# A routed attention kernel: the first block's rows turned after the last unit's first value products, and the routing probabilities stored as 18 rows

## The chip, the cores and the metric

One Trainium2 chip, one of its cores. The metric is device microseconds of one execution. The kernel before takes 1200.1 us, the median of three runs (1199.29 to 1203.38).

## What is computed

Three layers, one after the other, in float32: attention with pooled queries, a dense layer with a gate, and a routed layer with eight experts of which each token uses one.

```python
def _moe2_ref(x, w_gate, w_local, w1, w2):
    logits = np.einsum('bsd,de->bse', x, w_gate)
    local_gate = 1.0 / (1.0 + np.exp(-np.einsum('bsd,de->bse', x, w_local).squeeze(-1)))
...
            fresh_e = int(np.argmax(logits[b, s]))
            e = fresh_e if s == 0 or local_gate[b, s] < 0.5 else prev_e
...
            p = np.exp(logits[b, s] - logits[b, s].max())
            p /= p.sum() + 1e-09
            h = np.maximum(x[b, s] @ w1[e], 0.0)
            out[b, s] = p[e] * (h @ w2[e])
```

The input `x` has 4 x 576 = 2304 tokens of 512 numbers; an expert's matrices are 512 x 1024 and 1024 x 512. A token keeps the expert of the token before it where its local gate is open. `p[e]` is the routing probability that this case is about.

## The kernel before

**Stages.** Attention runs over 32 heads, to about 640 us. The dense layer works in nine units of 256 tokens (`u` from 0 to 8): `hidden` (the up products and the squares), `gate` (the sigmoid factor), `value` (the down products) and `product`, which multiplies the two and stores 128 rows of `x2d` in DRAM. Each matrix product is made of three passes over a high and a low half of its operands (`PASSES`). For each unit, `logits`, `route1`, `route2`, `route3` and `route4` find the expert of each token and scatter the token numbers into a table `tbl` in DRAM, one list for each expert; route4 issues two table scatters, each of which waits for the one before.

**Blocks.** The routed layer then works in blocks of up to 512 tokens of one expert. The numbers of a block's tokens are loaded from `tbl` (`load_ids`), their rows are gathered from `x2d` in two pairs of 128 (`gather_x`), turned on TensorE and split into high and low halves (`transpose_x`: 8 transposes, two copies on ACT at L1057 and two subtractions on DVE at L1058), taken through `up` and `down`, scaled with the tokens' probabilities (`gather_p` reads them from `pd` in DRAM into `pg`; `finish` does the scaling at L1093) and scattered to the output (L1094). Weights come in pieces of 512 KB (`load_w`) into a ring of raw buffers, three for the first block and five later, and are split by ACT and DVE (`split_w`, L1010 and L1011), which frees the buffer for a later piece. Block 0 belongs to the expert with the most tokens of units 0 to 6; it is chosen early (`early`, L1242), so that its rows and weights come while units 7 and 8 are still in the dense layer. The other blocks are known only after unit 8 has been routed (`block_list`, `block_list2`).

**Order.** The order on every engine is written out by hand: an engine works through its instructions in the order in which the program issues them. What matters here are the lines from L1288 on, for the last unit (u = 8). They issue `gate(u, 0)`, then `transpose_x(0)` for the first 256 rows of block 0 and `gather_x(0, 2)` for the other 256, which go into the same buffer `xg0`; then `route2` of unit 7, the first weight split, and `value(u, 0)` in two halves with `route3` of unit 7 between them. `product(u, 0)`, the second split, `gate(u, 1)` and `route4` of unit 7 follow, and then the rest of unit 8, between the up products of block 0. The second `transpose_x(0)` stands at L1330.

At L1349 `probabilities()` computes the probabilities of all 2304 tokens in one tile `pe`, 128 partitions x 18 columns (token 128 t + p stands in partition p, column t), and stores it at once to `pd`, which is in token order: every number is a piece of 4 bytes by itself. The store is issued on SP behind the first five weight pieces of block 1 and the two `load_ids` for blocks 1 and 2. On POOL the rows of block 1 are gathered next (L1350) and then the probabilities of block 0 (L1351, L1352), which wait for the store. On TensorE `down(0, 2)` and `down(0, 3)` stand before the second half of block 0, whose rows are up at L1378 (`pair_up`), whose first half is scaled at L1382, and whose down products are at L1390 (`pair_down`). In between `next_x(0)` turns the rows of block 1. All engines load eight numbers into registers at L1355 and L1356, and SP 20 more at L1358, before the sixth weight piece of block 1 is loaded.

Of the kernel before, what the change touches and what calls it, by code (L numbers as in the profile page):

```python
# [16 lines left out]
P = 128  # L17
# [20 lines left out]
def kernel(  # L38
# [16 lines left out]
    nc = tc.nc  # L55
# [4 lines left out]
    NTOK = B * T  # L60
# [3 lines left out]
    NT = NTOK // P  # L64
# [12 lines left out]
    pd = dram.tile([NTOK + 1, 1], F32, name="pd")  # L77
# [11 lines left out]
    ident = cp.tile([P, P], F32, name="ident")  # L89
# [103 lines left out]
    for i in range(2):  # L193
        t = s1.tile([P, KT, 192], F32, name=f"V{i}")
# [402 lines left out]
    for a in range(NH):  # L597
        e = a == NH - 1
# [11 lines left out]
    for t in range(NS + 23):  # L610
        h, kt = divmod(t, KT)
        p = h // 2
# [52 lines left out]
        if t == NS + 3:  # L665
# [5 lines left out]
            p1, p23 = [pm.tile([P, DM], F32, name=n) for n in ("p1", "p23")]  # L671
# [80 lines left out]
    def gate(u, i, p_r):  # L752
        a = AB[1][u % 2]
        s = slice(P * i, P * i + P)
        n = 0
        for c in range(4):
            for wl, xl in PASSES:
                nc.tensor.matmul(p_r, lhsT=a[:, xl, c, s], rhs=wr[:, wl, c], start=(n == 0), stop=(n == 11))
                n += 1
        RG[u, i] = u2.tile([P, DM], F32, name="r", bufs=4)  # L760
        nc.scalar.activation(out=RG[u, i], in_=p_r, func=AF.Sigmoid)

    def value(u, i, p_v, fs=range(8)):
        s = slice(P * i, P * i + P)
        for f in fs:
            for n, (wl, xl) in enumerate(PASSES):
                nc.tensor.matmul(  # L767
                    p_v, lhsT=SQ[u, f // 2][:, xl, f % 2, s], rhs=wv[:, wl, f],
                    start=(f == 0 and n == 0), stop=(f == 7 and n == 2),
                )  # L770

    def product(u, i, p_v):
        x2 = RG.pop((u, i))
        nc.vector.tensor_tensor(out=x2, in0=p_v, in1=x2, op=ALU.mult)
        t = 2 * u + i
        nc.sync.dma_start(x2d[P * t : P * t + P, :], x2)
        TT[u, i] = x2
# [49 lines left out]
    def route2(u):  # L827
        kg = KG.pop(u)
        p1r = p1.rearrange("p (j f) -> p j f", j=2)
        for j in range(2):  # L830
            for i in range(2):
                nc.tensor.matmul(
                    p1r[0:1, j, P * i : P * i + P], lhsT=kg[:, j, i : i + 1], rhs=identb, start=True, stop=True
                )
        kr = rp.tile([1, 2, 256], BF16, name="krow")
        nc.scalar.activation(out=kr, in_=p1r[0:1], func=AF.Copy)
        er = KG[u] = rp.tile([1, 256], BF16, name="erow", bufs=2)
        nc.vector.tensor_tensor_scan(
            out=er, data0=kr[:, 0], data1=kr[:, 1], initial=0.0 if u == 0 else carry[0][:, 255:256],
            op0=ALU.mult, op1=ALU.add,  # L840
        )
        carry[0] = er
# [138 lines left out]
    def load_w(s):  # L981
        j, c = divmod(s, 8)
        if j > JX:
            return
        e = regs[j][0]
        t = raws[s % NRAW if j else s % 3]
        if c < 4:
            nc.sync.dma_start(
                t.rearrange("p (c f) -> p c f", c=4),
                w1[bass.ds(e, 1), :, 256 * c : 256 * c + 256].rearrange("o (c p) f -> p (o c) f", p=P),  # L990
            )
        else:
            c -= 4
            nc.sync.dma_start(
                t.rearrange("p (c f) -> p c f", c=2),
                w2[bass.ds(e, 1), 256 * c : 256 * c + 256, :].rearrange("o (c p) f -> p (o c) f", p=P),
            )

    def split_w(s, eng=None):
        j, c = divmod(s, 8)  # L1000
        if j > JX:
            return
        t = raws[s % NRAW if j else s % 3]
        if c < 4:
            w = W1B[j % 2][:, :, c]
            t = t.rearrange("p (c f) -> p c f", c=4)
        else:
            w = W2B[j % 2][:, :, 2 * c - 8 : 2 * c - 6]
            t = t.rearrange("p (c f) -> p c f", c=2)
        nc.scalar.activation(out=w[:, 0], in_=t, func=AF.Copy)  # L1010
        (eng or nc.vector).tensor_tensor(out=w[:, 1], in0=t, in1=w[:, 0], op=ALU.subtract)  # L1011

    def load_ids(j):
        if j <= JX:
            nc.sync.dma_start(
                ids[j % 4], tbl[bass.ds(regs[j][1], 512), :].rearrange("(i p) o -> p (i o)", p=P),
                allow_slow_non_contiguous=True,
            )


    def gather_x(j, t):
        if j > JX:
            return
        for i in range(2):
            ix = bass.IndirectOffsetOnAxis(ap=ids[j % 4][:, t + i : t + i + 1], axis=0)
            if j:
                nc.gpsimd.indirect_dma_start(out=XGB[j % 2][:, i], out_offset=None, in_=x2d, in_offset=ix)
            else:
                nc.gpsimd.indirect_dma_start(
                    out=XGB[0][:, i], out_offset=None, in_=x2d[0 : 256 * (NU - 2)], in_offset=ix,  # L1030
                    bounds_check=256 * (NU - 2) - 1, oob_is_err=False,
                )

    def gather_p(j, t):
        for i in range(t, t + 2):
            ix = bass.IndirectOffsetOnAxis(ap=ids[j % 4][:, i : i + 1], axis=0)
            nc.gpsimd.indirect_dma_start(out=pgs[j % 2][:, i : i + 1], out_offset=None, in_=pd, in_offset=ix)  # L1037
# [7 lines left out]
    def transpose_x(j, b=0):  # L1045
        if j > JX:
            return
        xt = XT[j % 2]
        for c2 in range(2):
            pt = BK[b][0][c2]  # L1050
            for c in range(2):
                for i in range(2):
                    cc = 2 * c2 + c
                    nc.tensor.transpose(
                        pt[:, c, P * i : P * i + P], XGB[j % 2][:, i, P * cc : P * cc + P], ident
                    )
            nc.scalar.activation(out=xt[:, 0, 2 * c2 : 2 * c2 + 2], in_=pt, func=AF.Copy)  # L1057
            nc.vector.tensor_tensor(  # L1058
                out=xt[:, 1, 2 * c2 : 2 * c2 + 2], in0=pt, in1=xt[:, 0, 2 * c2 : 2 * c2 + 2], op=ALU.subtract
            )  # L1060
# [18 lines left out]
    def down(j, g, tiles=(0, 1)):  # L1079
        w, hs = W2B[j % 2], sq[g]  # L1080
        for i in tiles:
            n = 0
            for f in range(2):
                for wl, xl in PASSES:
                    nc.tensor.matmul(  # L1085
                        py[i], lhsT=hs[:, xl, f, P * i : P * i + P], rhs=w[:, wl, 2 * g + f],
                        start=(g == 0 and n == 0), stop=(g == 3 and n == 5),
                    )
                    n += 1
# [113 lines left out]
    def probabilities():  # L1203
        ls = rp.tile([P, NT, E], F32, name="ls")
        nc.vector.tensor_tensor(
            out=ls, in0=L[:, :, 0:E], in1=mx.unsqueeze(2).to_broadcast([P, NT, E]), op=ALU.subtract
        )
        nc.scalar.activation(out=ls, in_=ls, func=AF.Exp)
        sm = rp.tile([P, NT], F32, name="sm")
        nc.vector.tensor_reduce(out=sm, in_=ls, axis=AX.X, op=ALU.add)  # L1210
        nc.vector.tensor_scalar(out=sm, in0=sm, scalar1=1e-9, scalar2=None, op0=ALU.add)
        nc.vector.reciprocal(out=sm, in_=sm)
        nc.vector.tensor_tensor(out=ls, in0=ls, in1=oh, op=ALU.mult)
        pe = rp.tile([P, NT], F32, name="pe")
        nc.vector.tensor_reduce(out=pe, in_=ls, axis=AX.X, op=ALU.add)
        nc.vector.tensor_tensor(out=pe, in0=pe, in1=sm, op=ALU.mult)
        nc.sync.dma_start(
            pd[0:NTOK].rearrange("(t p) o -> p (t o)", p=P), pe, allow_slow_non_contiguous=True
        )


    def first_block():
# [64 lines left out]

    u = NU - 1  # L1288
    gate(u, 0, py[0])
    transpose_x(0)  # L1290
    gather_x(0, 2)
    route2(u - 1)
    split_w(0)
    load_w(3)
# [1 line left out]
    route3(u - 1)  # L1296
    value(u, 0, py[1], range(4, 8))
    product(u, 0, py[1])
    split_w(1)
    load_w(4)  # L1300
    gate(u, 1, py[0])
# [44 lines left out]
        load_w(s)  # L1346
    load_ids(1)
    load_ids(2)
    probabilities()  # L1349
    gather_x(1, 0)  # L1350
    gather_p(0, 0)  # L1351
    gather_p(0, 2)  # L1352
    down(0, 2)
    down(0, 3)
    n0 = nc.values_load(lst0[:, 2:3], min_val=0, max_val=512)  # L1355
    nk = [nc.values_load(nks[:, i : i + 1], min_val=0, max_val=JX) if i != 4 else None for i in range(8)]  # L1356
    for j in range(3, JX + 1):
# [103 lines left out]
```

## Time and profile before

| what | value |
|---|---|
| median of three runs | 1200.1 us |
| the profiled execution | 1199.74 us, its span 1198.0 us |
| mean granted TensorE clock | 0.972 of 2.4 GHz |
| busy in the span | TensorE matmul 1080.2 us (90%), DVE 828.2 (69%), ACT 718.6 (60%), POOL 575.3 (48%) |
| DMA | 156.31 MB in 147348 packets, 62993 of them under 512 bytes |

All starts are microseconds from the start of the span. PE is TensorE's matmul, PEld its weight load, DVE VectorE, ACT ScalarE, POOL GpSimd, SP SyncE. A row of a timeline has the start, the duration of the merged group, the engine, the line, the operation, the tiles as out<-in, the shape and the count; in brackets stands how long the engine was idle just before it and what ended that. Ends of matmuls are modelled and a group's end overlaps the next one's start a little, so differences of starts are the safer measure. A "q" behind an engine's name means its instruction queue. A row of a window has its bounds and length, the busy time (and instructions) of PE, PEld, DVE, ACT and POOL in this order, the granted clock, the DMA share and the GB/s. A granted clock of 1.00 is TensorE's level of 2.4 GHz, 0.50 that of 1.2 GHz.

### The profile page before, as it was taken

Reading aid. Unit: us, or ns where it says so; the run is one execution under the profiler, and the core shown is the slowest. Engines: PE = TensorE matmul, PEld = TensorE weight load, DVE = VectorE, ACT = ScalarE, POOL = GpSimd, SP = SyncE. Lnnn points to the kernel's source line nnn. Section 1 sums busy time; section 2 is a strip of 40 time slices with the busy share of each in tenths; the row PEclk is TensorE's granted clock in tenths of the full one; section 3 lists DMA queues with packets and bytes.
Section 4 is the critical chain, followed back from the end, with each engine's and each line's share of the span. In section 5 each row is a group of like instructions: output and inputs, shape, how many; then the busy total and the mean of one; then the engine's idle time right before and its main releaser. Section 6 shows DMA issues by size and latency. Waiting matters only on the chain. (4 is left out here: it accounts for less than half of the span.)

```text
span 1198.0 us, 18084 instructions
## 1 busy us (share of the span) xinstructions
PE 1080.2 (90%) x6073; PEld 910.6 (76%) x6073; DVE 828.2 (69%) x1255; ACT 718.6 (60%) x1006; POOL 575.3 (48%) x392
## 2 busy tenths in 40 slices
PE   7899999999999999978999989897987999998875
PEld 6677777777777777767887878776776888876764
DVE  6888888888888888889955665685353544446544
ACT  5787777777777777767775444341333535446543
POOL 2556666666666666468734333342213514144233
PEclk9999999999999999998999999998897999999988
DMA  9166666656566564515520322203646756556765
GB/s 198 32 132 148 138 142 141 140 130 131 131 149 141 137 138 100 157 45 172 182 98 10 36 31 32 36 18 89 117 81 153 253 178 202 176 179 213 251 205 176
DMA packets 147348, 156.31 MB, mean 130 GB/s; under 512 B 62993, under 2 KB 115857, under 8 KB 146324
## 3 DMA queue, kind: packets, MB, share of 16 engines
q1 hardware_dynamic: 140836, 141.51, 47.4%
q0 software_dynamic: 6384, 13.15, 3.7%
q8 instruction: 73, 1.20, 0.5%
q14 instruction: 55, 0.45, 0.1%
HBM read 107.30 MB, written 15.58 MB: 103 GB/s over the span
## 5 line engine op out<-in xcount | busy, mean ns | idle before, releaser
L403 PE MATMUL pvt<-sr,V 128*128 128x288 f32 x1152 | 328.5, 409 | 31.4 <-ACT xc L416 14.7
L403 PEld LDWEIGHTS pvt<-sr,V 128*128 128x128 f32 x1152 | 202.1, 190 | 71.2 <-POOL sr L389 17.9
L345 PE MATMUL pt<-kw 128*128 128x288 f32 x1152 | 247.3, 337 | 5.5 <-DVE Mt L357 4.1
L389 POOL TENSOR_TENSOR sr<-sr,Mb 128x576 f32<-128x576 f32 x96 | 142.5, 1487 | 195.3 <-ACT Mb L380 159.5
L357 DVE TENSOR_TENSOR Mt<-Mt,pt 128x576 f32<-128x576 f32 x224 | 168.1, 750 | 76.2 <-ACT sr L349 74.3
L349 ACT ACTIVATE sr<-pt 128x576 f32<-128x576 f32 x288 | 181.5, 646 | 54.6 <-PE pt L345 52.4
L345 PEld LDWEIGHTS pt<-kw 128*128 128x128 f32 x1152 | 177.6, 189 | 34.8 <-DVE Mt L357 10.4
L396 ACT ACTIVATE sr<-sr 128x1728 f32<-128x1728 f32 x96 | 157.9, 1644 | 52.0 <-DVE sr L390 46.4
L390 DVE TENSOR_TENSOR sr<-sr,Mb 128x1152 f32<-128x1152 f32 x96 | 160.9, 1676 | 2.8 <-ACT Mb L380 2.8
L727 PE MATMUL ph<-a,wk 128*128 128x256 f32 x864 | 108.4, 286 | 0.9 <-ACT kr L745 0.4
L727 PEld LDWEIGHTS ph<-a,wk 128*128 128x128 f32 x864 | 106.5, 193 | 2.6 <-ACT kr L745 1.0
L767 PE MATMUL py<-kw,sq 128*128 128x512 f32 x312 | 84.3, 423 | 0.0
L1068 PE MATMUL ph<-a,wk 128*128 128x256 f32 x576 | 73.4, 288 | 6.3 <-PEq L1415 5.8
L1085 PE MATMUL py<-kw,sq 128*128 128x512 f32 x324 | 78.3, 398 | 0.0
L1068 PEld LDWEIGHTS ph<-a,wk 128*128 128x128 f32 x576 | 71.3, 195 | 8.8 <-issue 7.7
L871 POOL DMA_INDIRECT tbl<-tid,si x18 | 18.4, 1021 | 122.9 <-DMA tbl<-tid,si 67.2
L745 ACT ACTIVATE kr<-ph 128x512 f32<-128x512 f32 x36 | 21.3, 592 | 92.4 <-PE ph L727 57.2
L446 POOL TENSOR_TENSOR xo<-xc,t 64x576 f32<-64x576 f32 x32 | 73.1, 2283 | 1.2
L783 DVE CUSTOM_DVE_ANT_0 a<-r,wg 128x512 f32<-128x512 f32 x96 | 71.4, 744 | 3.1
L767 PEld LDWEIGHTS py<-kw,sq 128*128 128x128 f32 x312 | 62.1, 203 | 15.0 <-issue 0.2
L1085 PEld LDWEIGHTS py<-kw,sq 128*128 128x128 f32 x324 | 60.8, 189 | 14.5
L1037 POOL DMA_INDIRECT pg<-pd,ids x44 | 44.4, 1009 | 37.4 <-DMA pg<-pd,ids 15.7
(250 smaller groups left out, 1756.7 us busy)
## 6 DMA issues: line engine op xcount, KB each, us to landing
wraw<-in_moe_w_dram SPq DMA_DIRECT2D x101, 512.0 KB
kw<-Hk SPq DMA_DIRECT2D x224, 72.0 KB
ql<-in_q_dram SPq DMA_DIRECT2D x16, 576.0 KB
kl<-in_k_dram SPq DMA_DIRECT2D x64, 144.0 KB
V<-in_v_dram SPq DMA_DIRECT2D x128, 72.0 KB
kw<-Hq SPq DMA_DIRECT2D x112, 72.0 KB
kw<-kw SPq DMA_DIRECT2D x14, 576.0 KB
xTd<-xo SPq DMA_DIRECT2D x16, 288.0 KB
```

The costliest lines, as they stand in the source:

```text
L345: nc.tensor.matmul(pt[:, i, :HT], lhsT=lhs, rhs=qh[:, hl, hd, i, :], start=(hl == 0), stop=(hl == 1))
L349: nc.scalar.activation(out=Sg[h, kt], in_=ptt[h, kt][:, :, :HT], func=AF.Copy)
L357: nc.vector.tensor_tensor(out=Mt[h], in0=a, in1=pt[:, :, :HT], op=ALU.max)
L389: nc.gpsimd.tensor_tensor(out=s[:, 0], in0=s[:, 0], in1=Mb[h], op=ALU.subtract)
L390: nc.vector.tensor_tensor(out=s[:, 1:3], in0=s[:, 1:3], in1=Mb[h].unsqueeze(1).to_broadcast([P, 2, T]), op=ALU.subtract)
L396: nc.scalar.activation(out=s, in_=s, func=AF.Exp, scale=scale)
L403: nc.tensor.matmul(pvt[h][:, i, :HT], lhsT=V[(h // 2) % 2][:, kt, c : c + P], rhs=Sg[h, kt][:, i], start=(kt == 0), stop=(kt == KT - 1),)
L446: nc.gpsimd.tensor_tensor(out=xo[p].rearrange("p (i t c) -> p i c t", i=2, c=9)[a], in0=y[a], in1=t2[a], op=ALU.mult)
L727: nc.tensor.matmul(pt[:, i], lhsT=wk[:, wl, g, c, P * i : P * i + P], rhs=a[:, xl, c], start=(n == 0), stop=(n == 11))
L767: nc.tensor.matmul(p_v, lhsT=SQ[u, f // 2][:, xl, f % 2, s], rhs=wv[:, wl, f], start=(f == 0 and n == 0), stop=(f == 7 and n == 2),)
L1068: nc.tensor.matmul(pt[:, i], lhsT=w[:, wl, g, c, P * i : P * i + P], rhs=x[:, xl, c], start=(n == 0), stop=(n == 11))
L1085: nc.tensor.matmul(py[i], lhsT=hs[:, xl, f, P * i : P * i + P], rhs=w[:, wl, 2 * g + f], start=(g == 0 and n == 0), stop=(g == 3 and n == 5),)
```

## The change

`transpose_x(0)` and `gather_x(0, 2)` of the last unit move from behind `gate(u, 0)` to behind `product(u, 0)`, ahead of the second weight split. `probabilities()` only computes; a new function `store_p` turns the 128 x 18 tile on TensorE to 18 rows of 128, copies them from PSUM (`p23`) into a part of the tile `ls` that is free by then, and stores 18 rows of 512 bytes. It is issued behind `down(0, 3)`, and the two `gather_p` behind it; their order on POOL's queue, after `gather_x(1, 0)`, stays.

```diff
--- before.py
+++ after.py
@@ -1214,9 +1214,14 @@
         pe = rp.tile([P, NT], F32, name="pe")
         nc.vector.tensor_reduce(out=pe, in_=ls, axis=AX.X, op=ALU.add)
         nc.vector.tensor_tensor(out=pe, in0=pe, in1=sm, op=ALU.mult)
-        nc.sync.dma_start(
-            pd[0:NTOK].rearrange("(t p) o -> p (t o)", p=P), pe, allow_slow_non_contiguous=True
-        )
+        return pe, ls
+
+
+    def store_p(pe, ls):
+        nc.tensor.transpose(p23[0:NT, 0:P], pe, ident)
+        row = ls.rearrange("p t e -> p (t e)")[0:NT, 0:P]
+        nc.vector.tensor_copy(row, p23[0:NT, 0:P])
+        nc.sync.dma_start(pd[0:NTOK].rearrange("(t p) o -> t (p o)", p=P), row)
 
 
     def first_block():
@@ -1287,8 +1292,6 @@
 
     u = NU - 1
     gate(u, 0, py[0])
-    transpose_x(0)
-    gather_x(0, 2)
     route2(u - 1)
     split_w(0)
     load_w(3)
@@ -1296,6 +1299,8 @@
     route3(u - 1)
     value(u, 0, py[1], range(4, 8))
     product(u, 0, py[1])
+    transpose_x(0)
+    gather_x(0, 2)
     split_w(1)
     load_w(4)
     gate(u, 1, py[0])
@@ -1346,12 +1351,13 @@
         load_w(s)
     load_ids(1)
     load_ids(2)
-    probabilities()
+    pe, ls = probabilities()
     gather_x(1, 0)
+    down(0, 2)
+    down(0, 3)
+    store_p(pe, ls)
     gather_p(0, 0)
     gather_p(0, 2)
-    down(0, 2)
-    down(0, 3)
     n0 = nc.values_load(lst0[:, 2:3], min_val=0, max_val=512)
     nk = [nc.values_load(nks[:, i : i + 1], min_val=0, max_val=JX) if i != 4 else None for i in range(8)]
     for j in range(3, JX + 1):
```

## Rows read from the trace of the kernel before

**Rows 1.** Windows, routed stage: busy us by engine (instructions), clock, DMA share, GB/s.
```profile
930.00:1092.00 162.00, 157.57 (x947) 137.19 (x945) 81.22 (x88) 79.47 (x107) 60.23 (x54) 1.00 0.61 195
1092.00:1198.00 106.00, 76.90 (x433) 64.79 (x432) 53.05 (x54) 50.80 (x65) 34.85 (x31) 0.93 0.69 214
```

**Rows 2.** PE's timeline, 827 to 850: start, us, line, tiles, count, idle before.
```profile
827.29 2.93 PE L758 MATMUL py<-wr,a 128*128 128x512 f32 x12
837.23 0.45 PE L1054 MATMUL ptx<-ident,xg 128*128 128x128 f32 x1 [7.00 <-DMA xg<-x2d,ids]
837.95 1.75 PE L1054 MATMUL ptx<-ident,xg 128*128 128x128 f32 x7 [0.28 <-DMA xg<-x2d,ids]
...
845.10 3.07 PE L767 MATMUL py<-kw,sq 128*128 128x512 f32 x12
848.00 2.91 PE L758 MATMUL py<-wr,a 128*128 128x512 f32 x12
```

**Rows 3.** DVE's timeline: `kg` of unit 7, and the last step of the probabilities.
```profile
829.90 0.16 DVE L825 SCALAR_TENSOR_TENSOR kg<-kg,f 128x2 bf16<-128x2 bf16 x1
...
885.79 0.18 DVE L1216 TENSOR_TENSOR pe<-pe,sm 128x18 f32<-128x18 f32 x1
```

**Rows 4.** POOL's timeline, 829 to 834: the first block's gather and two splits.
```profile
829.49 1.03 POOL L1029 DMA_INDIRECT xg<-x2d,ids  x1 [8.61 <-issue]
...
831.85 2.48 POOL L748 TENSOR_TENSOR sq<-kr,sq 128x512 fp32r<-128x512 f32 x2
```

**Rows 5.** PE's timeline, 888 to 923: the first block's second half.
```profile
888.00 5.91 PE L1068 MATMUL p<-a,wk 128*128 128x256 f32 x48
899.44 8.73 PE L1068 MATMUL p<-a,wk 128*128 128x256 f32 x48 [5.53 <-DVE kw L1075]
912.87 0.45 PE L1054 MATMUL ptx<-ident,xg 128*128 128x128 f32 x1 [4.70 <-DMA xg<-x2d,ids]
...
915.53 2.93 PE L1085 MATMUL py<-kw 128*128 128x512 f32 x6
918.25 4.82 PE L1085 MATMUL py<-kw,sq 128*128 128x512 f32 x18
```

**Rows 6.** ACT's timeline, 896 to 916.
```profile
896.47 1.06 ACT L1010 ACTIVATE w1b<-wraw 128x1024 fp32r<-128x1024 f32 x1 [4.12 <-DMA wraw<-in_moe_w_dram]
...
908.21 0.60 ACT L1074 ACTIVATE sq<-p 128x512 fp32r<-128x512 f32 x1 [2.65 <-PE p L1068]
914.79 0.69 ACT L1093 ACTIVATE a<-py,pg 128x512 f32<-128x512 f32 x1 [5.98 <-DMA pg<-pd,ids]
```

**Rows 7.** POOL's timeline, 901 to 913: block 1's row gather, then `pg`.
```profile
901.72 0.98 POOL L1027 DMA_INDIRECT xg<-x2d,ids  x1 [14.24 <-DMA ids<-tbl]
903.00 0.96 POOL L1027 DMA_INDIRECT xg<-x2d,ids  x1 [0.30 <-issue]
912.06 0.94 POOL L1037 DMA_INDIRECT pg<-pd,ids  x1 [8.10 <-DMA pd<-pe]
```

**Rows 8.** SP's queue, 850 to 921: weight loads and the store of `pd`.
```profile
850.05 5.53 SPq L994 DMA_DIRECT2D wraw<-in_moe_w_dram  x3
...
897.25 0.50 SPq L1217 DMA_DIRECT2D pd<-pe  x1
915.50 4.76 SPq L994 DMA_DIRECT2D wraw<-in_moe_w_dram  x3
```

**Rows 9.** Windows of 5 us: columns as in rows 1.
```profile
830.00:835.00 5.00, 0.22 (x1) 0.00 (x0) 0.06 (x1) 0.60 (x1) 4.00 (x4) 0.89 0.95 283
915.00:920.00 5.00, 4.89 (x14) 3.59 (x14) 2.65 (x4) 4.48 (x7) 2.47 (x3) 0.57 0.71 217
```

**Rows 10.** POOL's timeline, 852 to 863: unit 7's two table scatters.
```profile
852.14 1.03 POOL L871 DMA_INDIRECT tbl<-tid,si  x1 [9.61 <-DVE base L869]
862.00 0.97 POOL L871 DMA_INDIRECT tbl<-tid,si  x1 [8.83 <-DMA tbl<-tid,si]
```

**Rows 11.** Line L1356 on PE's weight queue: durations in ns, first and last start.
```profile
L1356 PEldq TENSOR_LOAD <-nks x7: 300/307/315, 884.4 to 886.9; - x7
```

## Prediction

> **What bounds the kernel now.** I read the windows view of the last stage first, to see whether time won earlier reaches the end. From 930 to 1092 us PE is busy 157.57 of 162 us at the full clock (1.00, the 2.4 GHz level), so there it is the bound; from 1092 on it is busy 76.90 of 106 and shares the bound with DMA (share 0.69) [rows 1]. The weight loads of this stage go into five buffers that are freed by splits which ACT and DVE do between PE's groups, so the stream follows PE. Hence what PE gains ahead of 930 should mostly be seen at the end.
>
> Next, PE's timeline at the two edits. At 830.22 (827.29 + 2.93) the gate product of the last unit ends and PE stands 7.00 us until 837.23 for the rows of the first block, then 0.28 for their second half; gate(u, 1) comes only at 848.00 [rows 2]. Nothing else was missing: `kg`, which route2 needs, was done at 830.06 (829.90 + 0.16) [rows 3], and the low halves of the squares that value(u, 0) needs come from POOL at 831.85 plus 2.48, that is 833.1 and 834.3 [rows 4]. The stall is one of order alone: PE takes its instructions in sequence, and the one that waits is at the head.
>
> The second place: PE ends the first block's up products at 908.17 (899.44 + 8.73), waits 4.70 for the rows of block 1, and starts the down product (L1085) at 915.53 [rows 5]. ACT is then waiting too: L1093 starts at 914.79 after 5.98 for `pg` [rows 6]. On POOL the row gather of block 1 was issued at 901.72 and 903.00, and the gather of `pg` only at 912.06, after 8.10 for `pd<-pe` [rows 7]. The store was issued on SP at 897.25 [rows 8], so the `pd` write takes 912.06 - 897.25 = 14.8 us from issue to its waiter, for 9 KB written as 2304 separate words of 4 bytes; and the row gather, issued in the middle of it, lands only when it is over (11.15 us for the first half, 912.87 - 901.72).
>
> **Part 1, the turn of the first block's rows.** Moved: 8 transposes (PE), 2 L1057 (ACT), 2 L1058 (DVE), 2 gathers (POOL). After the change PE goes from 830.2 to route2 (0.4), 12 value products (2.9 at full clock: 845.10 to 848.00 [rows 2]), route3 (0.15) and 12 more, and is at the transposes at about 836.6. The squares hold nothing up: those of group 3, ready at 834.3, are wanted from about 835.3. The rows land as before, 837.23 and 837.95, so PE still waits about 1.1 us in all, then turns for 1.75 [rows 2] and starts gate(u, 1) at 839.7 instead of 848.00: 8.3 us. If the clock, which has no long pause before it now, stays at the full level, the 7 transposes take half of 1.75 and the gain is 9.1. The other end: split_w(0) is no longer behind the turn, so load_w(3) can start sooner, while the rows are in flight; its 512 KB at the 283 GB/s of that stretch [rows 9] would delay them by 1.8, leaving 6.5. As the load comes behind two stores on the same queue I take 8.5.
> On the queues: ACT has split_w(0) and DVE `erow`, split_w(0), `oh` and the product ahead of the turn's copies now. A wait for the first weights there is covered until 838; uncovered, each us of it delays split_w(1) and the sigmoid of gate(u, 1) by one. SP gets nothing moved past it. POOL issues the second pair of gathers at 839.0 to 839.7, as now, after the turn has read the buffer; they are wanted only at L1330, behind unit 8's routing. The table scatter of unit 7, now at 852.14 [rows 10], comes to stand right behind them at about 843.6. All later work (unit 8, routing, block list, the loads of block 1) hangs on gate(u, 1) and moves with it.
>
> **Part 2, the probabilities.** Removed: the store of 2304 words. Added: one PE transpose (some 0.25, as one of the 7 in 1.75 [rows 2]), one DVE copy (about 0.2, like L1216's 0.18 [rows 3]) and a store of 18 rows of 512 bytes. I cost the first two at nothing. PE waits for `pe` (done 885.97 [rows 3]) and for down(0, 3), which ends where L1068 starts, at 888.00 [rows 5]; the 7 register loads behind it on the weight queue (now 884.4 to 887.2 [rows 11]) come late, so L1068 may start some 1.3 later (885.97 and the 2.8 that the loads take, and the step between). Cover: the next L1068 stands until 899.44 for DVE (5.53 idle [rows 5]), set by ACT, which waits for weights until 896.47 [rows 6]. Without this cover the 1.3 would be paid. DVE's copy ends near 889; the split behind it is of weights that ACT gets no sooner than now. SP stands until the scatter before `ids` is done, so the store still goes at 897.25, and nothing on SP waits for it longer than now.
> The store itself: no row shows it. Above, 14.8 us as now; below, the 2.73 from a `pg` gather's issue to its user (912.06 to 914.79 [rows 6, 7]), as few bytes. I take the low end, since the number of packets falls from 2304 to 18. It then lands by about 900 to 901, behind the loads, ahead of the `pg` gathers that follow the row gathers on POOL (904.3, 905.5, ...).
> The row gather without the store: between 2.73 and the 7.74 of the first block's (829.49 to 837.23 [rows 2, 4]), which had 2 MB of loads and stores ahead at a DMA share of 0.95 [rows 9]. Here SP issues nothing from 897.25 to 915.50 [rows 8], so the low half is nearer: both halves land by 908.17. Then PE turns the rows at once, to 909.2; ACT scales the first result at 908.81 (the end of L1074, 908.21 + 0.60) to 909.5; L1085 starts at 909.5 instead of 915.53: 6.0. Beside it the clock: L1085's first 24 products took 7.5 us (915.53 to 918.25 + 4.82) against 5.8 at the full clock (twice 2.9), at a granted clock of 0.57 in 915 to 920 [rows 5, 9], after PE had idled 4.70. PE would now come to them from 9 us of work, so I add 1.5: 7.5 in all. With the gather at 7.74 (910.7 for its second half) L1085 starts at 911.8 and the clock may fall again: 3.7.
>
> **Sum.** 8.5 + 7.5 = 16.0. What is late next is the weight stream: load_w(13) follows SP's register loads at 915.50 [rows 8] and moves by part 1 alone. Block 1's last weights are needed at its down product, 7 us or more later than they then land, so I take off 0.5. 1199.74 - 15.5 = 1184.2; the median of the three runs is 0.36 above the profiled one, so **1184.6**.
>
> The Trainium skill, page "DMA: Bandwidth & Descriptors", section "Queues, rings and completion order", says that each DMA engine goes round its queues packet by packet, so a gather in another queue should not have to wait for a whole store; by that the 11.15 us of the gather would be its own, and the sum would be 8.5. The row on which I lean is that it lands as the store ends; this gives the first rival its chance.
>
> **Rivals.** (a) The gather is slow by itself, or the first products wait for another thing in the same place (ACT's splits behind load_w(13)). Then L1085 stays near 915.5 in old time, part 2 gives 0 to 3, and the time is 1188 to 1191.5. For: no row shows a gather of 512 KB on idle DMAs. Against: 7.74 with the DMAs full. 0.17.
> (b) Part 1 is half given back in the block's weights: load_w(4) (850.05 now, 2.1 ahead of the scatter at 852.14 [rows 8, 10]) comes to stand beside the second gathers and the scatter. If it lands 8 late, ACT stands in split_w(4) and up(0, 1) follows; after some slack 3 to 5 of the 8.5 are lost: 1187.5 to 1189.5, or 1192 if all of part 1 goes. Against: loads and scatters meet in the kernel before as well. 0.12.
> (c) Slower: the four table scatters of units 7 and 8 run one after the other (each waits for the one before: 852.14, and 862.00 after 8.83 for it [rows 10]), and the first will follow the gathers on POOL's queue directly. They set `ids`, and with it the rows of block 1. It decides where they stretch by more than 16 us in sum, 4 each on the 9.9 from one to the next; each us beyond costs one, from 19.6 on the kernel is slower by over 3.6, and at 21 in sum the time is 1205. Against: in the kernel before they meet two stores and weight loads too and keep to 9.9. 0.03.
> (d) The edits do what they say but the words come out as they were (the 18 rows still split into 4-byte packets): as (a), 1191; in its share.
>
> **How the numbers follow.** Forecast (1181 to 1188) 0.62, (a) 0.17, (b) 0.12, (c) 0.03; for 0.06 both parts are given back by something not seen here. Over 0.3% is 3.6 us, about what a measurement of this kernel tells from no change. Faster: 0.62 + 0.17 + 0.12 = 0.91; same 0.06; slower 0.03. The range: the best ends are 9.1 + 7.5 = 16.6, and runs spread by some 2, so 1180.5; above, each part alone: 1192, with 1 for its bounds, 1193.
>
> **What would show it.** Right: no PE wait over 1.5 us between L758's first end and the transposes; gate(u, 1) 8 to 9 us earlier; `pg`'s first gather about 1.25 after the second row gather; L1085 within 2 us of the end of the up products and at full clock. Part 1 is wrong if PE waits as long at split_w or at up(0, 0 to 3) instead; part 2 if the transposes of L1054 still wait for `xg`; the sum if 930 to 1092 shows new gaps.

## The result and the profile after

The changed kernel takes 1183.77 us, the median of four runs (1182.8 to 1188.92), against 1199.69 (1199.13 to 1203.38) for the kernel before: ratio 0.987, interval 0.9834 to 0.9905. Two later sets, on two more chips, gave 0.9872 (0.9824 to 0.992) and 0.9873 (0.9839 to 0.9908). 1184.6 was forecast. The profiled execution took 1182.80 us, its span 1181.0, 17.0 less than before. Ratios below come from undisturbed runs on one chip, so they are not always the quotient of two medians.

**The first edit.** PE's timeline of the changed kernel, to be held beside [rows 2]:

```profile
824.46 2.93 PE L758 MATMUL py<-wr,a 128*128 128x512 f32 x12
...
831.69 0.20 PE L849 MATMUL p<-onesb,erow 1*128 1x8 bf16 x2 [1.02 <-DVE erow L838]
831.82 3.06 PE L767 MATMUL py<-kw,sq 128*128 128x512 f32 x12
834.72 1.24 PE L1054 MATMUL ptx<-ident,xg 128*128 128x128 f32 x8
835.72 3.00 PE L758 MATMUL py<-wr,a 128*128 128x512 f32 x12
```

The turn is now one group of 8 transposes with no bracket: PE waits for no row. From the first L758 to gate(u, 1), the second, it is 11.26 us (835.72 - 824.46); before it was 20.71 (848.00 - 827.29). POOL's timeline shows the gathers and scatters around it, and below them those of the second place [rows 4, 7, 10]:

```profile
826.19 1.03 POOL L1029 DMA_INDIRECT xg<-x2d,ids  x1 [8.89 <-issue]
...
839.94 1.03 POOL L871 DMA_INDIRECT tbl<-tid,si  x1 [1.49 <-DVE base L869]
849.29 0.97 POOL L871 DMA_INDIRECT tbl<-tid,si  x1 [8.32 <-PE ptx L793]
...
888.14 0.98 POOL L1027 DMA_INDIRECT xg<-x2d,ids  x1 [13.40 <-DMA ids<-tbl]
889.42 0.96 POOL L1027 DMA_INDIRECT xg<-x2d,ids  x1 [0.30 <-issue]
890.68 0.94 POOL L1037 DMA_INDIRECT pg<-pd,ids  x1 [0.30 <-issue]
```

**The second edit.** The gather of `pg` follows the row gather at once, where it had waited 8.10 for the store. PE's timeline [rows 5]:

```profile
868.43 0.24 PE L1194 MATMUL p<-key,eo 40*1 40x12 f32 x4
...
882.92 6.01 PE L1068 MATMUL p<-a,wk 128*128 128x256 f32 x48 [0.56 <-DVE kw L1075]
891.80 0.30 PE L1054 MATMUL ptx<-ident,xg 128*128 128x128 f32 x1 [2.87 <-DMA xg<-x2d,ids]
893.74 1.75 PE L1054 MATMUL ptx<-ident,xg 128*128 128x128 f32 x7 [1.64 <-DMA xg<-x2d,ids]
895.14 2.91 PE L1085 MATMUL py<-kw 128*128 128x512 f32 x6
897.85 4.89 PE L1085 MATMUL py<-kw,sq 128*128 128x512 f32 x18
...
915.74 1.70 PE L1129 MATMUL p<-ident,kr 128*128 128x128 f32 x8 [1.83 <-ACT kr L1124]
...
926.61 11.76 PE L1068 MATMUL ph<-a,wk 128*128 128x256 f32 x96 [1.44 <-PEq L1421]
```

The rows' first half is in PE 3.66 us after its issue (891.80 - 888.14) instead of 11.15, and L1085 starts 7.00 after that issue (895.14 - 888.14) instead of 13.81. But PE still stands twice, 2.87 and 1.64, and the first 24 products of L1085 still take 7.44 us (897.85 + 4.89 - 895.14): the windows view grants half the clock there, the lower of the two levels [rows 9].

```profile
895.00:898.00 3.00, 3.00 (x10) 2.42 (x9) 1.99 (x3) 3.00 (x5) 1.40 (x2) 0.50 0.24 86
```

The waits in the last two rows have grown. The kernel before has them too, but short; its timeline of PE, with the block list (L1194):

```profile
882.12 0.24 PE L1194 MATMUL p<-key,eo 40*1 40x12 f32 x4
...
934.99 0.65 PE L1129 MATMUL p<-ident,kr 128*128 128x128 f32 x4 [0.31 <-ACT kr L1124]
...
942.98 11.77 PE L1068 MATMUL ph<-a,wk 128*128 128x256 f32 x96 [0.52 <-PEq L1415]
```

ACT stands too in the changed kernel; its timeline:

```profile
893.94 0.69 ACT L1093 ACTIVATE a<-py,pg 128x512 f32<-128x512 f32 x1 [4.38 <-DMA pg<-pd,ids]
...
905.47 1.06 ACT L1010 ACTIVATE w2b<-wraw 128x1024 fp32r<-128x1024 f32 x1 [6.32 <-DMA wraw<-in_moe_w_dram]
```

That weight piece is the first that SP asks for after its register loads, at 901.74 in SP's queue [rows 8]:

```profile
884.19 0.46 SPq L1224 DMA_DIRECT2D pd<-ls  x1
901.74 2.21 SPq L994 DMA_DIRECT2D wraw<-in_moe_w_dram  x3
```

**The account of the 17.0 us**, by differences of starts: 2.83 had been won ahead of the change (L758 at 824.46 for 827.29), 9.45 by the first edit, 1.41 from gate(u, 1) to the block list (L1194, 882.12 and 868.43), 6.70 from there to L1085 (33.41 and 26.71). 4.02 went back from L1085 to the up products of block 2 (27.45 and 31.47), and 0.6 came behind them (255.0 and 254.4 to the end). The 2.83 and the 1.41 are spread between traces and not the change: over the thirteen traces of this document the first L758 starts at 823.71 to 829.12, and from gate(u, 1) to L1194 it is 32.6 to 34.6, in no order of the kernels.

### The profile page after: what moved, and what is told of

The parts are those of the page before. It is cut to its first block, busy times and chain, and to the rows that moved or that the text cites. A ratio compares the mean times of both kernels' runs of the same rounds, so it can differ in the third digit from the quotient of the medians.

```text
span 1181.0 us, 18087 instructions
## 1 busy us (share of the span) xinstructions
PE 1076.5 (91%) x6074; PEld 907.7 (77%) x6074; DVE 836.4 (71%) x1256; ACT 718.8 (61%) x1006; POOL 577.1 (49%) x392
## 2 busy tenths in 40 slices
DMA packets 145055, 156.31 MB, mean 132 GB/s; under 512 B 60682, under 2 KB 113564, under 8 KB 144031
## 5 line engine op out<-in xcount | busy, mean ns | idle before, releaser
L1068 PE MATMUL ph<-a,wk 128*128 128x256 f32 x576 | 71.8, 284 | 7.5 <-PEq L1421 6.7
L1085 PE MATMUL py<-kw,sq 128*128 128x512 f32 x324 | 78.4, 398 | 0.0
L1068 PEld LDWEIGHTS ph<-a,wk 128*128 128x128 f32 x576 | 69.8, 191 | 9.9 <-issue 8.9
L1085 PEld LDWEIGHTS py<-kw,sq 128*128 128x128 f32 x324 | 60.9, 189 | 14.5
```

The source lines that it names most:

```text
L1068: nc.tensor.matmul(pt[:, i], lhsT=w[:, wl, g, c, P * i : P * i + P], rhs=x[:, xl, c], start=(n == 0), stop=(n == 11))
L1085: nc.tensor.matmul(py[i], lhsT=hs[:, xl, f, P * i : P * i + P], rhs=w[:, wl, 2 * g + f], start=(g == 0 and n == 0), stop=(g == 3 and n == 5),)
```

## The experiments

Two readings of each trace carry the comparison: G, from the first L758 to gate(u, 1), and R, from the issue of block 1's row gather to L1085. B is from L1085 to block 2's first L1068, S how long after L1085's start SP asks for weight piece 13, W what PE waits at L1129 (us, one trace each; the words are 4-byte pieces). Each ratio is to runs of the kernel before on the same chip. Expected times were given from the first chip; in the three later sets the kernel before takes 1197.9, 1204.5 and 1205.2 us in the median, so what is compared with them is the ratio.

| kernel | ratio (interval) | G | R | B | S | W |
|---|---|---|---|---|---|---|
| before | 1 | 20.71 | 13.81 | 27.45 | -0.03 | 0.31 |
| changed | 0.987 (0.9834 to 0.9905) | 11.26 | 7.00 | 31.47 | 6.60 | 1.83 |
| turn alone | 0.993 (0.990 to 0.996) | 11.04 | 16.82 | 28.05 | -4.95 | 0.31 |
| rows alone | 0.9957 (0.9932 to 0.9982) | 19.55 | 7.03 | 28.43 | 6.13 | 1.53 |
| changed + unread words | 0.9923 (0.9894 to 0.9952) | 12.01 | 12.61 | 28.19 | -0.04 | 0.31 |
| first weights behind the turn | 0.9886 (0.9844 to 0.9927) | 11.46 | 7.09 | 30.03 | 5.51 | 2.88 |
| turn alone, words behind the rows | 0.9967 (0.9935 to 0.9999) | 11.18 | 19.93 | 31.70 | -8.91 | 0.31 |
| changed, second set | 0.9872 (0.9824 to 0.992) | 11.97 | 7.02 | 35.16 | 10.01 | 4.47 |
| registers 8 to 12 later | 0.9859 (0.9813 to 0.9906) | 11.01 | 10.82 | 26.85 | -0.32 | 0.31 |
| registers 3 to 12 later | 0.9901 (0.9867 to 0.9936) | 11.02 | 10.86 | 30.83 | -10.12 | 0.31 |
| changed, third set | 0.9873 (0.9839 to 0.9908) | 11.39 | 6.98 | 34.46 | 10.85 | 5.12 |
| L1085 first | 0.9913 (0.988 to 0.9947) | 13.33 | 7.41 | 29.22 | 5.07 | 1.48 |
| L1085 first, registers later | 0.9868 (0.9833 to 0.9902) | 11.46 | 7.45 | 30.54 | -0.36 | 1.60 |

### Each edit alone

The kernel before with the turn moved, and with the words made rows:

```diff
     product(u, 0, py[1])
+    transpose_x(0)
+    gather_x(0, 2)
     split_w(1)
```

> The kernel before with the turn of the first block's rows moved, and the store of words left. Theory (the stall was one of order, and the two parts add up): TensorE's 7.00 us wait ahead of the transposes is gone, gate(u, 1) comes 8.5 to 9.5 us earlier behind the end of the first gate product, the later wait for block 1's rows (4.70) stays or grows, and the time is 1190.5, between 1189 and 1192. Rival (one part carries it all, because both end at the same later wait): the wait for block 1's rows grows by the whole gain and the time is within 3 us of 1199.7.

> The kernel before with the probabilities turned and stored as 18 rows, and the turn of the first block's rows left in its place. Theory: the 7.00 us wait stays; the row gather of block 1 lands 4 to 6 us after its issue instead of 11, the gather of the probabilities is issued 1.25 us behind the second row gather, L1085 starts 5 to 8 us earlier, some 2 us of which the weight stream takes back; 1193.5, between 1191.5 and 1195.5. Rival (the gather is slow by itself): L1085 within 2 us of its place, 1198 or more.

G falls where the turn is moved, R where the words are rows, and neither with the other edit (with the turn alone R even grows, to 16.82). The times came out as expected, and the traces but for some tenths (20.71 - 11.04 = 9.67 earlier for 8.5 to 9.5, 3.65 to land for 4 to 6). By the ratios the turn is worth 0.70%, 8.4 of 1199.7 us (4.8 to 12.0), the rows 0.43%, 5.2 (2.2 to 8.2); their sum, 13.6, is not to be told from the 15.6 of both. In the trace with rows alone PE has the old stall and the fast gather; its timeline:

```profile
836.49 0.44 PE L1054 MATMUL ptx<-ident,xg 128*128 128x128 f32 x1 [6.65 <-DMA xg<-x2d,ids]
...
902.90 0.42 PE L1054 MATMUL ptx<-ident,xg 128*128 128x128 f32 x1 [3.45 <-DMA xg<-x2d,ids]
```

The gather had been issued at 899.25, 3.65 before the second row.

### Do the words hold the row gather, or is it slow by itself?

The changed kernel with a second store, of the same 2304 words, to a place that nothing reads, right behind the one of 18 rows:

```diff
         nc.sync.dma_start(pd[0:NTOK].rearrange("(t p) o -> t (p o)", p=P), row)
+        nc.sync.dma_start(pd2.rearrange("(t p) o -> p (t o)", p=P), pe, allow_slow_non_contiguous=True)
```

> The changed kernel with one store more: the same 2304 words of 4 bytes go from the tile pe to a spare place in DRAM that nobody reads, issued on SP right behind the 18 rows. The output is the same. Theory (the words block the DMA engines for whoever shares them): the probabilities are ready as now, yet block 1's row gather lands 10 to 11 us after its issue instead of 4, L1085 starts 6 to 8 us later, and the time is 1189 to 1191.5. Rival (the gather takes its turn beside the words, and only the wait for the probabilities counted): the row gather within 1.5 us of now, the time within 1 us of the changed kernel's 1183.8.

The lines below L78 have a number higher by one here, and those behind the added store by two. POOL's and PE's timelines, and ACT's:

```profile
895.76 0.98 POOL L1028 DMA_INDIRECT xg<-x2d,ids  x1 [15.38 <-DMA ids<-tbl]
...
898.30 0.94 POOL L1038 DMA_INDIRECT pg<-pd,ids  x1 [0.30 <-issue]
```

```profile
906.07 0.45 PE L1055 MATMUL ptx<-ident,xg 128*128 128x128 f32 x1 [7.02 <-DMA xg<-x2d,ids]
```

```profile
907.19 0.69 ACT L1094 ACTIVATE a<-py,pg 128x512 f32<-128x512 f32 x1 [5.96 <-DMA pg<-pd,ids]
```

No instruction waits for the spare words, yet the rows take 10.31 us (906.07 - 895.76) and `pg` 8.89 (907.19 - 898.30), which had been asked for without a wait. So the store of the words holds both gathers, and the ratio, 0.9923, is that of the turn alone: what the rows bring is the absence of this store. L1085 is 5.61 later than in the changed kernel, a little less than expected.

The words do not do this by standing ahead of the gather on the DMAs. Windows of this run, and below them one of the changed kernel (columns as in [rows 1]):

```profile
896.00:898.00 2.00, 2.00 (x19) 2.00 (x18) 0.69 (x1) 0.60 (x1) 1.70 (x2) 1.00 0.00 0
898.00:904.00 6.00, 1.05 (x9) 0.85 (x8) 0.69 (x1) 0.60 (x1) 3.78 (x4) 0.89 0.51 25
904.00:907.00 3.00, 0.48 (x2) 0.22 (x2) 0.00 (x0) 0.00 (x0) 0.00 (x0) 0.50 0.67 128
...
889.00:893.00 4.00, 0.30 (x1) 0.14 (x1) 0.69 (x1) 0.56 (x1) 2.96 (x4) 0.90 0.45 129
```

By the profile the last packet of the words has ended by 896, and until 898 no queue has any packet. The gather, asked for at 895.76 and 897.04, then runs at 25 GB/s until 904, with the DMAs busy at a share of 0.51, and only behind that at 128, the rate that it has from the start in the changed kernel. The kernel before shows the same: no more than 15 small packets from 902.10 to 904, the gather at 22 GB/s from 904 to 910, and `pg`, which waits for the store, at 912.06. So the store goes on holding others for some 8 us after its own packets; what they wait for then isn't shown.

### Is it enough that the rows land early?

The turn alone, with the words stored from POOL's queue behind the row gather:

```diff
     gather_x(1, 0)
+    store_w(pe)
     gather_p(0, 0)
```

> The turn alone, with the store of 2304 words taken from SP to POOL's queue, behind block 1's row gather. Theory (the words do two things, they slow the row gather and they keep the probabilities back, and either alone holds L1085): the rows land 4 to 5 us after their issue and TensorE turns them at the end of the up products, but the probabilities come 15 us or more after the words' issue, L1085 waits for ACT's scaling some 3 us longer than with the turn alone, 1192.5 to 1198 against its 1191.0. Rival (the row gather alone counts): L1085 6 us earlier, about 1186.

POOL's, ACT's and PE's timelines:

```profile
885.98 0.98 POOL L1027 DMA_INDIRECT xg<-x2d,ids  x1 [13.64 <-DMA ids<-tbl]
...
900.59 1.01 POOL L1037 DMA_INDIRECT pg<-pd,ids  x1 [11.06 <-DMA pd<-pe]
```

```profile
905.17 0.69 ACT L1093 ACTIVATE a<-py,pg 128x512 f32<-128x512 f32 x1 [14.13 <-DMA pg<-pd,ids]
```

```profile
892.23 0.98 PE L1054 MATMUL ptx<-ident,xg 128*128 128x128 f32 x7 [1.72 <-DMA xg<-x2d,ids]
905.91 2.93 PE L1085 MATMUL py<-kw 128*128 128x512 f32 x6 [12.70 <-issue]
```

The rows are there by 892.23, and L1085 starts at 905.91, 0.74 after ACT's scaling of the first result, which frees the buffer that it writes (the trace of the turn alone has the same 0.74, and names ACT's L1093 as what L1085 waits for). R is 3.11 more than with the turn alone, as expected. It is not enough that the rows land: the words delay L1085 through the rows or through `pg`, and only the removal of both helps. Here too the DMAs stand while the store is out: from 892 to 899 they move one packet, and `pg` has `pd` at 900.59.

### Do the first weights take part 1 back?

```diff
     route2(u - 1)
-    split_w(0)
-    load_w(3)
...
     gather_x(0, 2)
+    split_w(0)
+    load_w(3)
     split_w(1)
```

> The changed kernel, but the first weight split and the load behind it stay behind the turn of the rows, as they were, so that the turn passes the two halves of the value products alone. Theory (only TensorE's order counts): gate(u, 1) as early as in the changed kernel, the load some 4 us later without a wait for it, the time within 1 us of 1183.8. Rival (part of the gain came from the first weights being split sooner): TensorE waits at the first up products or at the block's down products for 3 us or more, 1186.5 or more.

G is 11.46 for 11.26, and the ratio, 0.9886, is that of the changed kernel within the intervals: no cost of the earlier load_w(3) to the turn, and no gain from the earlier split, is seen. (The time, 1186.0 by the ratio, lies between the theory's 1184.8 and the rival's 1186.5, so it does not decide by itself; waits of 3 us or more at the first up products or the down products, which the rival named, are not in the trace.) A by-product is the clock. Here the up products ended only 1.94 us before L1085, with no stall of more than 0.6 between, and the first 24 products took 5.84 us (897.67 + 4.37 - 896.20); PE's timeline:

```profile
895.67 0.66 PE L1054 MATMUL ptx<-ident,xg 128*128 128x128 f32 x4 [0.56 <-DVE sq L1075]
896.20 1.64 PE L1085 MATMUL py<-kw 128*128 128x512 f32 x6
897.67 4.37 PE L1085 MATMUL py<-kw,sq 128*128 128x512 f32 x18
```

The granted clock is 1.00 from 896 to 902 here. So the 1.5 us of the clock exist; the changed kernel, where PE has idled 4.51 in two pieces, has 0.50 and doesn't collect them.

### What takes time back behind L1085?

In the changed kernel SP loads the registers of ten blocks, 20 loads one after the other, ahead of weight piece 13. In the next two kernels those of blocks 8 to 12, or of all from 3 on, are loaded two blocks ahead of their use:

```diff
-    for j in range(3, JX + 1):
+    for j in range(3, 8):
...
     def block(j):
+        if 7 < j + 2 <= JX:
+            block_regs(j + 2, lst[:, 0, j + 1 : j + 2], lst[:, 1, j + 1 : j + 2])
         load_ids(j + 2)
```

> The changed kernel once more, as the base for the others of this group. All theories: 1182.5 to 1187, and its distance to the kernel before within 2 us of the sum of the two parts measured alone (6.9 and 4.2).

> The changed kernel, but SP loads the registers of blocks 8 to 12 two blocks ahead of each one's use instead of all at once, so that the sixth weight piece of block 1 (the one that waits for SP's register loads) is issued some 6 us sooner, when the row gather has landed. Theory (the weight stream, held by SP's register loads, takes back part of what TensorE gained): ACT's waits for the raw weights at L1010 in block 1 (9.8 us in the changed kernel) fall by 5 or more, TensorE's wait at L1129 (1.83) is gone, the time is 1.5 to 3 us under the changed kernel of this group. Rival (these waits are ACT's and DVE's, not TensorE's): within 0.7 us of it.

> The changed kernel, with the registers of all blocks from 3 on loaded two blocks ahead of use, so that the sixth to eighth weight pieces of block 1 are issued some 12 us sooner, beside the row gather. Theory (the row gather suffers from what else the DMA engines carry): the waits for raw weights are gone, but the rows land 6 to 8 us after their issue instead of 4, L1085 comes 2 to 3 us later, and the time is within 1.5 us of the changed kernel's and above that of registers_half. Rival (the gather takes its turn): the rows land as now, and the time is as registers_half or lower.

The base missed its expectation: its median, 1189.48, is above 1182.5 to 1187, and 15.0 below the kernel before on that chip where 11.1 within 2 was expected, the sum of the medians of the two parts alone. As the runs of the changed kernel spread by 16.5 on that chip, this doesn't show that the parts do not add up.

Columns S and W tell what is late. Piece 13 keeps its place behind the block list (33.4 us after L1194 before, 33.3 after), while L1085 has moved ahead. In the two repeated sets it comes even later, 36.0 and 37.3 after L1194, because SP takes 3.1 and 3.6 us more from the store to this piece in these traces, over its register loads. Where SP asks for it no later than L1085 starts, PE waits 0.31 at L1129 for ACT; where it asks 5.5 to 6.6 later, 1.5 to 2.9; at 10 to 11, 4.5 to 5.1. (The last two kernels of the table have another order here, with the turn and its copies between, and don't follow this.) The third set's trace shows the chain on SP, ACT and PE:

```profile
910.28 2.21 SPq L994 DMA_DIRECT2D wraw<-in_moe_w_dram  x3
```

```profile
914.09 1.06 ACT L1010 ACTIVATE w2b<-wraw 128x1024 fp32r<-128x1024 f32 x1 [10.62 <-DMA wraw<-in_moe_w_dram]
```

```profile
922.96 1.95 PE L1129 MATMUL p<-ident,kr 128*128 128x128 f32 x8 [5.12 <-ACT kr L1124]
```

W is not all of what goes back. B is 4.02, 7.71 and 7.01 longer in the three traces of the changed kernel than before, and W is 1.83, 4.47 and 5.12; behind it PE's transposes run slower (8 in 1.7 to 1.9 us for 1.06), and PE waits 1.44, 1.97 and 1.49 for its own queue where it waited 0.52. Counted from L1194 to block 2's L1068, the kernel before needs 60.86 and the changed one 58.18, but 61.13 and 60.93 in the repeated sets: in those two traces nothing of the 6.7 won at L1085 is left there, while the one with rows alone keeps 5.2 (55.63).

With half of the registers later the wait is gone, and B (26.85) is no longer than in the kernel before. The time is not measurably better, 0.9859 against 0.9872. Part of the gain was lost ahead of L1085: ACT's last L1074 starts 4.64 us after PE's end by the profile (896.28 for 891.64), released by something that the trace only calls remote, and R is 10.82. ACT's timeline:

```profile
896.28 0.60 ACT L1074 ACTIVATE sq<-p 128x512 fp32r<-128x512 f32 x1 [6.89 <-remote]
...
904.79 1.06 ACT L1010 ACTIVATE w2b<-wraw 128x1024 fp32r<-128x1024 f32 x1 [1.52 <-DMA wraw<-in_moe_w_dram]
```

Most of the rest is lost in block 2, where PE now waits in the up products: from L1194 to block 2's first L1085 it is 73.04 us, and 73.90 in the changed kernel of this set. PE's timeline:

```profile
933.80 7.50 PE L1068 MATMUL ph<-a,wk 128*128 128x256 f32 x48 [2.52 <-DVE kw L1075]
```

With all registers later, the weights come at 889.28, beside the row gather of 888.54, whose halves then land 5.88 and 7.68 us after issue; and PE stands 3.96 for its own queue at block 2's L1068. The rows land as the theory said; L1085 comes 3.84 later and not 2 to 3, with ACT's last L1074 late here as well (897.25, 3.64 after PE's end). That kernel's ratio is 0.9901, not to be told from 0.9872: no use of so early a start is seen. What PE's queue waits for there isn't shown (4.25 in the kernel with the words behind the rows, whose registers load as before).

### A version that should beat both

Since PE waits for rows while L1085's operands are there, L1085 of the first result tile goes ahead of the turn, and the first gather of `pg` ahead of that of the rows; the second version has the later registers besides.

```diff
+    gather_p(0, 0)
     gather_x(1, 0)
-    gather_p(0, 0)
     gather_p(0, 2)
...
+            for g in range(4):
+                down(0, g, (0,))
...
     next_x(0)
```

> The changed kernel as it is, as the base for the two versions beside it. Both theories: 0.987 of the kernel before, and PE standing 4 to 5 us in two pieces between the end of the first block's up products and L1085, with L1085's first 24 products at 7 to 7.5 us.

> The changed kernel with two reorderings: the first gather of probabilities goes ahead of the row gather of block 1, and the first tile's down products of the first block's second half (L1085) go ahead of the turn of block 1's rows. Theory (what is left of the stall is order alone again, PE standing at transposes for rows while L1085's operands are there): L1085 starts within 2 us of the end of the up products instead of 6.2 us, its first 24 products take about 6 instead of 7.4, and the time falls 4 to 6 us below the changed kernel (ratio to the kernel before about 0.982 to 0.984), less what the weight stream takes back, which could be 1 to 3. Rival (the words' removal has moved the bound to the stream of weights and to SP's register loads): L1085 starts earlier but the next up products (L1068 of block 2) do not, and the time is within 1 us of the changed kernel.

> As the version with L1085 first, and besides the registers of blocks 8 to 12 are loaded two blocks ahead of their use rather than all at once ahead of the weights of slots 13 to 15. Theory (both the order of PE and SP's register loads cost): from L1085 to L1068 of block 2 about 27 us, as in the kernel before, against 31 to 35 in the changed one; the time 5 to 8 us below the changed kernel (ratio about 0.980 to 0.983), and 1 to 3 below the version without the registers. Rival (the take-back is not the register loads): no difference from the version without the registers.

The base has the expected ratio, and its PE stands 3.74 in two pieces (4 to 5 was expected). Neither version beats it: 0.9913 and 0.9868 against 0.9873 (the first is probably slower, but the intervals overlap). PE no longer waits for rows, but L1085 came 3.68 and 4.27 us behind the up products, not 2, for ACT; PE's and ACT's timelines of the first version:

```profile
905.61 2.44 PE L1085 MATMUL py<-kw 128*128 128x512 f32 x6 [3.67 <-ACT a L1093]
```

```profile
904.38 0.60 ACT L1074 ACTIVATE sq<-p 128x512 fp32r<-128x512 f32 x1 [5.00 <-remote]
```

The up products, too, ended later behind L1194 (25.92 and 23.85 us, 20.87 in the third set), since ACT had their weights later; nothing in these edits is ahead of those loads. From L1194 to block 2 the traces have 58.82 and 58.66 against 60.93, a gain of 2 us that the time doesn't show.

## Why the prediction was right, and where it was not

**Bound and order (right).** The stall at the first edit was one of order alone: with the turn moved the same rows cost no wait, and all that hangs on gate(u, 1) moves with it (L1194 by 13.69, gate(u, 1) by 12.28, 2.83 of each from ahead of the edit). In this pair what was won by block 2 stayed: from its L1068 to the end it is 255.0 and 254.4. Over all traces that stretch takes 254.4 to 260.5, so a single pair can't show more than that.

**Part 1 (right; 8.5 of 6.5 to 9.1).** 9.45 in the pair of traces, a little above the range, and 8.4 by the time of the turn alone. The wait of 1.1 that the sum kept is not there: the gather starts 1.73 us after L758 instead of 2.20, and `erow` held PE for 1.02 on the way. The transposes ran at the full clock, as the high end had it (1.24 for 8).

**Part 2, the store and the gather (right in mechanism and size).** 6.0 was taken. At a fixed issue of the row gather, L1085 is 6.81 earlier (13.81 and 7.00), and this repeats in every kernel with rows (6.98 to 7.09 where ACT is not held) and none with words. The store is off the path, as the low end had it, and the gather took 3.66 and 4.32, in the lower half of 2.73 to 7.74. The 1.3 that PE's register loads were to cost is there (1.77 idle for issue at 876.35 ahead of the first L1068) and was covered.

**The clock's 1.5 (wrong).** The step that failed is "PE would now come to them from 9 us of work". The up products ended earlier as well: their second pair, which had waited 5.53 for weights, waited 0.56 and ran at the full clock (6.01 for 8.73), since ACT had weight piece 9 at 7.0 us after SP began to ask for pieces 8 to 11, and not at 10.1. Whether this comes of the change isn't shown: the wait is 0.56 to 1.32 in the three traces of the changed kernel and 0.80 with rows alone, and 2.5 to 3.7 in the eight others. Thus the up products and L1085 lie 6.21 us apart, with 4.51 of it idle for rows, nearly as in the kernel before (7.36, with 5.05). So the sign that the prediction named, L1085 within 2 us of the up products and at the full clock, did not come, and the gain is 0.1 (7.54 and 7.44); the 5.84 of the kernel with the first weights behind the turn shows that the size was right for a PE that hardly stands.

**What is late next (mis-sized).** The weight stream was named, with 0.5 us. From L1085 to block 2, 4.02 went back in the first pair, and 7.71 and 7.01 in the two repeated sets, against the one trace of before; the part of it that is PE's wait behind the weights is W, 1.83 to 5.12. What failed is "needed at its down product, 7 us or more later than they then land": piece 13 moves by part 1 alone, as said, but PE doesn't wait for the weights, it waits for L1124 behind their split on ACT. ACT is free for the piece from 899.15, 2.6 us before SP asks for it, and has it at 905.47. The rest, PE's slower stretch behind that wait and its longer wait for its own queue, stood in no term of the sum, and the cause of the latter stays open.

**The sum.** 15.5 was forecast; the three sets give 1.30, 1.28 and 1.27%, 15.6 to 15.2 us. That it fits so well is in part luck. In the profiled pair 1.4 too much for the clock and 3.5 too little for what goes back behind L1085 stand against 0.9 and 0.8 too little in the two parts, and against 2.83 ahead of the change and 1.41 behind gate(u, 1) that have nothing to do with it. In the traces of the repeated sets all of part 2 has gone back by block 2, and yet their times fit as well; where these runs make it good isn't shown.

**Rivals.** (a), that the gather is slow by itself, and (d) fall: 3.61 to 4.98 us from its issue to PE's first transpose wherever the words are rows, no weights load beside it and the turn comes first; and the profile's page counts 60682 packets under 512 bytes for 62993 before, so the words are gone. The Trainium skill, page "DMA: Bandwidth & Descriptors", section "Queues, rings and completion order", says that each DMA engine goes round its queues by packets; the prediction drew from it that the gather would keep its 11.15 us. That conclusion fails: in the run with unread words the gather takes 10.31 us in a queue other than the words' against 3.66, and the measurement decides. The rule itself isn't tested by it, as no packet of the words is left when the gather's begin. (b) falls by L1194, which keeps all of gate(u, 1)'s gain. (c) falls: the scatters of unit 7 start 9.35 us apart (839.94 and 849.29), 9.86 before.

## What to carry to other kernels

Price a store in 4-byte pieces by measuring who else's transfers are on the DMAs until it has landed, not by its bytes, its packets or its own waiter alone: here turning 9 KB on TensorE cost a transpose and a copy and brought L1085 forward by 6.8 us. When a wait goes, list what was hidden behind it with a time of its own (here SP's register loads ahead of the weights), and count from where that starts instead of granting it the same slack. Ask of any clock gain whether the engine still stands ahead of it.

## What was not expected of the hardware

2304 words of 4 bytes, 9 KB, lengthened the first half of a gather of 512 KB in another queue from 3.66 to 10.31 us, more than weight pieces of 512 KB beside it did (5.88 for its first half, 7.68 for its second), and did so after their own packets were over, with the gather at 25 GB/s for 129. ACT's last L1074 of the up products sometimes starts 1.6 to 4.6 us after PE's end by the profile, with the releaser given as remote; it is in the traces of five of the kernels run (both with later registers, both with L1085 first, and the one with unread words) and in none of the three of the changed kernel at that place. Its cause stays open, and with it whether these versions lose to it by their edits or by chance. Open, too, is why one kernel's runs spread by up to 16.5 us on one chip (1181.45 to 1197.96 in the second set).
